# An adaLN attention block: the last V product moved behind the first attention step's scores, the first score tile on other banks, three paired maxima taken singly

## The chip, the core and the metric

The kernel runs on one core of one Trainium2 chip. The time is device time in microseconds (us) for one execution of the whole program, and it is compared as the median of several executions. TensorE, VectorE, ScalarE and GpSimd compute, SyncE (SP) issues most of the transfers. TensorE writes into PSUM, which has eight banks; each 128 x 512 tile of fp32 takes one bank.

## The reference, cut to what matters

```python
# x: 1 x 2048 x 448, 16 heads of 28, feed-forward width 1792, fp32
mod = silu(c) @ w_mod                      # -> sa, ca, ga, sb, cb, gb
h = layernorm(x) * (1 + ca) + sa
q, k, v = split(h @ wqkv)                  # 16 heads
p = softmax((q @ k^T) * 28 ** -0.5)
x = x + ga * ((p @ v) @ wo)
h = layernorm(x) * (1 + cb) + sb
h = gelu(layernorm(h) @ w1 + b1) @ w2 + b2
out = x + gb * h
```

## The kernel before, in words

All products that need more precision than one pass gives are split into a high and a low part, and three of the four part products are summed in PSUM.

**Projection stage** (the loop over `b` from L600). The 2048 tokens are taken in four blocks of 512. For each block a list of tasks is worked off in order: Q and K products of a group of four heads (`qk_task`, L336) and four V products of 128 tokens each (`v_task`, L368), eleven matmuls each (`mm_acc`, L315 to L317). The products write to two PSUM banks named `pa`; ScalarE copies the result out. For the last block (b = 3) the list has six Q and K tasks and then four V products.

**Row maxima.** The softmax takes from each score a bound of its row's maximum, and these maxima are computed ahead, by 32-row matmuls of Q against a chunk of K into banks named `mx` (`max_mm`, L387) with a VectorE reduce for each (`max_one`, L395 to L397). For head group 0 and the later query blocks two key chunks are done as a pair (`pair_diff`, L401): one matmul against the difference of the chunks, a ScalarE Relu (L405), one matmul against the first chunk, and one fused VectorE operation (L409). `emit_task` (L503) puts some of these behind every product of the projection stage: `p1_n` (L526, set in L615 to L621) says how many operations, whether a sixth bank is used, and how many pairs. In the last block each of the first five tasks has one pair at most, each later one three, and nothing is put behind the last V product (L616, L617). All pairs must be done by L677.

**Banks at the handover.** In the projection stage the pool `ps1` holds 2 `pa`, 5 `mx` and 1 `o` bank. It is closed in L680; then the accumulator `o` of attention gets a pool of its own (L683), and `share(3, 2)` (L692) opens a pool with three `mx` banks and two score tiles `s` of two banks each. On SP's queue stand at this place the stores of the last Q and K parts, the loads of the keys of head group 0 (`load_k`, L573), loads of the next group's Q and K (`load_hi`, L416) and of `wo`.

**Attention** (the loop from L1024). Sixteen units (four head groups, four query blocks) of sixteen steps (key tiles of 128). A step makes the scores of four heads in two halves, each into a score tile (L1047), with some maxima between (`emit_max`, L492; four and three in turn in most steps); ScalarE's exponential (L1052) writes them into `pt`, which lies in the slots `c0`, `c1`, `d0` in turn (L1022). The product with V of the step before follows (`av`, L1014 to L1017). The slots `c0` and `c1` held the split input of block 3 in the projection stage, and `d0` the Relu results.

After attention come the output projection's rest and the feed-forward part (L1080 on), which the change doesn't touch.

Of the kernel before, what the change touches and what calls it, by code (L numbers as in the profile page):

```python
# [16 lines left out]
ALU = mybir.AluOpType  # L17
AX = mybir.AxisListType
PSUM = bass.MemoryType.PSUM
# [22 lines left out]
def tile_adaln_block(ctx: ExitStack, tc: tile.TileContext, x, wqkv, wo, w1, b1, w2, b2, c, w_mod, out):  # L42
# [17 lines left out]
    def sbt(tag, shape, dt=F32, bufs=1):  # L60
        return sb.tile(shape, dt, tag=tag, name=nm(tag), bufs=bufs)
# [17 lines left out]
    def ps_s():  # L79
        return psp[0].tile([128, 512], F32, tag="pa", name=nm("pa"), bufs=2)  # L80

    def ps_mx():
        return psp[0].tile([128, 512], F32, tag="mx", name=nm("mx"), bufs=psp[1])
# [281 lines left out]

        return split

    def v_task(b, t):  # L368
        p = ps_s()
        ts = slice(t * 128, (t + 1) * 128)  # L370
        hh, hl = hT[b]
        mm_acc(p[:, :D], terms448(
            lambda k: hh(k)[:, ts], lambda k: hl(k)[:, ts], lambda k: wv[0][:, k, :], lambda k: wv[1][:, k, :],
        ))
        emit_task(*p1_n)
        act.copy(v_sb[b][:, t, :, :DH], p[:, :D].rearrange("p (h d) -> p h d", d=DH))


# [8 lines left out]
    def max_mm(g, qt, i, j, k, ps=None):  # L387
        if (g, qt) not in mxp:
            mxp[(g, qt)] = sbt("mxp", [128, 4, 4, 4], bufs=6)
        m = (ps or ps_mx)()  # L390
        js = slice(32 * j, 32 * j + 32)
        pe.matmul(m, qh_sb[(g, qt)][js, i * 128 : (i + 1) * 128], k[js, :], start=True, stop=True)  # L392
        return m
# [30 lines left out]

    def max_fin(g, qt):
        m32 = sbt("m32", [128, 32], F32R, bufs=2)
        c0 = 1 if (g, qt) in paired else 0
        pool.memset(f(m32)[:, 16:32], 0.0)
        dve.tensor_reduce(
            out=m32[:, 0:16].rearrange("p (h i) -> p h i", i=4),  # L430
            in_=mxp[(g, qt)][:, :, :, c0:].rearrange("p i h c -> p h i c"), op=ALU.max, axis=AX.X, negate=True,
        )

        def put():
            r = sbt("full", [128, 512], F32R, bufs=3)[:, :32]
            dve.transpose(f(r), f(m32))
            dst = f(qst[g * NB + qt])[DH:128:32, 0, :].rearrange("j (i b q) -> j i b q", b=4, q=32)
            for b in range(4):
                sp.dma_start(dst[:, :, b, :], f(r)[32 * b : 32 * b + 16, :])

        late.append([2, put, g * NB + qt])
# [158 lines left out]
    for b in range(NB):  # L600
        more = b + 1 < NB
        tasks = []
        for g in range(1 if b else 0, NG):
            tasks += [(b, 0, g), (b, 1, g)]
        if b == 0:
            tasks[1], tasks[2] = tasks[2], tasks[1]
        tasks += [(b, 2, t) for t in range(4)]
        if more:
            stages, later = stages[-4:] if b else stages, ln1_stages(b + 2) if b + 2 < NB else None
            xs_next = []  # L610
            tasks[10:10] = [(b + 1, 0, 0), (b + 1, 1, 0)]
        for n, (tb, kind, g) in enumerate(tasks):
            post = []
            ready, newq = newq, []
            p1_n[0] = P1RATE if b < 1 else P1RATE + 1  # L615
            if not more and n == len(tasks) - 1:  # L616
                p1_n[0] = 0  # L617

            k = n - (5 if b < 2 else 4)
            p1_n[1] = not (more and (0 <= k < NC)) and not (b == 1 and n < 4)  # L620
            p1_n[2] = (3 if n > 4 else 1) if b == 3 else 2 if b == 2 and p1_n[1] else 1  # L621
            if kind < 2:
                fn = qk_task(tb, kind, g, 6, firsts[n]) if b == 0 and n < 2 else qk_task(tb, kind, g)
                if g == 0:
                    fn()
                else:
                    post.append(fn)
                if kind == 1 and (g == 0 or (g == 1 and tb < 2)):
                    newq = [(g, qt, cch) for qt in range(tb + 1) for cch in range(tb + 1) if max(qt, cch) == tb]
            else:  # L630
                v_task(tb, g)
            for item in ready:
                queue_max(*item)
            if b == 0 and 2 <= n < 6:
                prep_w(2, n - 2, act.copy, dve)
            if more:
                k = n - (5 if b < 2 else 4)
                if b == 0 and n < 4:
                    for fn in stages[2 * n : 2 * n + 2]:
                        fn(xs_next)  # L640
                if b and n < 4:
                    stages[n](xs_next)
                if 0 <= k < NC:
                    post.append(h_chunk(b + 1, xs_next, k))
                if later and 8 <= n < 12:
                    later[n - 8](None)
            if n == 6:
                v_init(b)
                if b == 0:
                    mod_load(0)  # L650
                    mod_load(1)
            if b == 2 and n == 5:
                sp.dma_start(b1_col, b1.rearrange("(k p) -> p k", p=128))
            if b == 1:
                if n < 2:
                    mod_mm(n)
                    mod_load(2 + n)
                elif n in (2, 3):
                    mod_mm(n)
                    if n == 3:  # L660
                        mod_fin()
            if not more:
                if n == 0:
                    load_q(0)
                    load_q(1)
                if n == 5:
                    load_k(0, 0)
                if n == 6:
                    act.activation(cols[:, 0:1], zero_col, AF.Exp)
                    for ch in range(1, 4):  # L670
                        load_k(0, ch)
            tick_late()
            for fn in post:
                fn()
        if more:
            stages = later
    assert not pxq  # L677
    finish_max(0, 0)
    tick_late(True)
    ps1_cm.__exit__(None, None, None)  # L680


    o_pool[0] = ctx.enter_context(tc.tile_pool(name="po", bufs=1, space=PSUM))  # L683
    shared = []

    def share(n_mx, n_s):
        if shared:
            shared.pop().__exit__(None, None, None)
        shared.append(tc.tile_pool(name=nm("ps"), bufs=1, space=PSUM))
        psp[:] = [shared[0].__enter__(), n_mx, n_s]  # L690

    share(3, 2)  # L692

    phase1[0] = False
    for item in deferred:
# [323 lines left out]
                start=(kt == 0), stop=(kt == NKT - 1),  # L1019
            )  # L1020

    ptags = ["c0", "c1", "d0"]  # L1022
    done_max = set()
    for u in range(NU):  # L1024
        g, qt = divmod(u, NB)
        for kt in range(NKT):
            step = u * NKT + kt
            if kt == 1 and u + 1 < NU and u + 1 not in qst:
                load_q(u + 1)
            if kt == NKT - 6 and u + 1 < NU:  # L1030
                finish_max(*divmod(u + 1, NB))
            tick_late()
            if not (three or mxq or late):
                three = True
                share(1, 3)
            pt = slot(ptags[step % 3], [128, 4, 512], F32)
            n = n_maxima(step)
            n0 = 1 if n == 3 and step % 4 == 3 else 2

            ks, qs = kst[(g, kt // 4)], qst[u]  # L1040
            kc = slice((kt % 4) * 128, (kt % 4 + 1) * 128)
            for hf in range(2):
                s2 = ps_s2()
                for term, (kp, qp) in enumerate(((0, 0), (1, 0), (0, 1))):
                    for jj in range(2):
                        rows_ = slice(64 * hf + 32 * jj, 64 * hf + 32 * jj + 32)
                        pe.matmul(s2[:, jj, :], ks[rows_, kp, kc], qs[rows_, qp, :], start=(term == 0), stop=(term == 2))  # L1047
                    if hf == 0 and term < min(n0, n):
                        emit_max(1, 1)
                    if hf == 1 and ((term == 0 and n - n0 > 0) or (term == 2 and n - n0 > 1)):  # L1050
                        emit_max(1, 0)
                act.activation(pt[:, 2 * hf : 2 * hf + 2, :], s2, AF.Exp, scale=SCALE)  # L1052
            if pend is not None:
                pu, pkt, pp, po = pend
                av(pu, pkt, pp, po)
                if pkt == NKT - 1:
                    end_unit(pu, po)
            if kt == 0:
                o = ps_o()
            pend = (u, kt, pt, o)  # L1060
            if qt == NB - 1 and kt % 4 == 3 and g + 1 < NG:
                load_k(g + 1, kt // 4)
            for fn in sched.pop(step, ()):
                fn()
# [90 lines left out]
```

## Time and profile before

| | us |
|---|---|
| median of 3 runs | 1147.98 |
| the runs | 1146.90 to 1148.01 |
| the profiled execution's own time | 1149.55 |
| its span in the profile | 1147.7 |
| TensorE busy in it | 1136.2 |
| mean granted clock of TensorE | 0.997 |

The profile is of one execution. Its lines name engine, line of the kernel, operation, and tiles as output <- input; a group has its count behind an x. "Granted clock" is the share of full speed at which TensorE was let run. In an excerpt in order of time the first column is the start in us from the span's start, the second the length of the group, and in brackets stands idle time before it and what ended that.

### The profile page before, as it was taken

The numbers are of one execution on the slowest core, as the hardware profiler recorded it, in microseconds if no ns is written. First come the engines' busy times: TensorE is split into PE (matmuls) and PEld (weight loads), VectorE is DVE, ScalarE is ACT, GpSimd is POOL, SyncE is SP. The second block draws the span as 40 slices with busy tenths as digits, with TensorE's granted clock in tenths as the row PEclk, the third lists the DMA queues.
The fourth block names the chain that finished last, engine by engine and source line by source line (L and its number), as shares of the span: only waits on it lengthen the run. The fifth ranks groups of instructions, "written<-read, shape, count | busy, mean of one in ns | idle before, by whom it ended". The sixth has DMA issues, their size and how long they took to land.

```text
span 1147.7 us, 20818 instructions
## 1 busy us (share of the span) xinstructions
PE 1136.2 (99%) x8380; PEld 683.8 (60%) x8380; DVE 829.7 (72%) x1487; ACT 682.5 (59%) x839; POOL 216.1 (19%) x232
## 2 busy tenths in 40 slices
PE   8999999999999999999999999999999999999998
PEld 6767765444444444444444444545458888888887
DVE  6868786999999999899999876585438853444322
ACT  4656757778777787878778777675862321211110
POOL 2533431210000000000000011207214503123000
PEclk9999998999999999999999999999999999999999
DMA  9643354121222111222111221020413100000000
GB/s 298 203 145 110 111 178 136 37 56 49 62 75 78 59 47 38 76 75 66 51 44 40 83 84 60 26 84 1 126 55 95 42 33 1 1 33 1 33 1 33
DMA packets 51377, 81.08 MB, mean 71 GB/s; under 512 B 12728, under 2 KB 21772, under 8 KB 51280
## 3 DMA queue, kind: packets, MB, share of 16 engines
q1 hardware_dynamic: 50656, 79.01, 21.8%
q8 instruction: 66, 1.08, 0.4%
q0 software_dynamic: 336, 0.28, 0.1%
q10 hardware_dynamic: 288, 0.46, 0.1%
q14 instruction: 31, 0.25, 0.1%
HBM read 53.11 MB, written 26.35 MB: 69 GB/s over the span
## 4 chain that ended last, share of the span: by engine, by line
PE 96%; DMA 1%; ACT 1%; DVE 1%; issue 0%; DVEq 0%; SPq 0%; ACTq 0%
PE s L1047 28%; PE o L1017 22%; PE mx L317 16%; PE pa L339 7%; PE mx L392 6%; PE s L1105 4%; PE s L1106 4%; PE s L1104 4%; PE pa L317 3%; DMA slot_v<-in_A_wqkv_dram 1%; PE o L240 1%; PE mx L240 1%; ACT slot_c L1052 0%; DMA acc<-in_A_x_dram 0%; PE o L547 0%
## 5 line engine op out<-in xcount | busy, mean ns | idle before, releaser
L397 DVE TENSOR_REDUCE mxp<-mx 128x1 f32<-128x512 f32 x919 | 580.7, 685 | 107.8 <-PE mx L392 103.8
L1047 PE MATMUL s<-slot_b,slot_a 32*128 32x512 f32 x3072 | 384.6, 424 | 1.8 <-ACT full L814 0.7
L1052 ACT ACTIVATE slot_c<-s 128x1024 f32<-128x1024 f32 x342 | 331.7, 1022 | 85.0 <-PE s L1047 84.8
L1047 PEld LDWEIGHTS s<-slot_b,slot_a 32*128 32x128 f32 x3072 | 216.8, 184 | 254.8 <-ACT slot_c L1052 150.8
L392 PE MATMUL mx<-kh,qh 32*128 32x512 f32 x899 | 290.4, 471 | 0.1
L1052 ACT ACTIVATE slot_d<-s 128x1024 f32<-128x1024 f32 x170 | 164.8, 1022 | 42.6 <-PE s L1047 42.5
L1017 PE MATMUL o<-slot_c,v 128*32 128x512 f32 x1368 | 184.4, 608 | 0.4 <-ACT osb L986 0.4
L1088 ACT ACTIVATE full<-mx,b_col 128x512 f32<-128x512 f32 x56 | 38.6, 689 | 192.0 <-PE mx L317 175.6
L1091 DVE CAST hi<-full 128x512 fp32r<-128x512 f32 x56 | 25.2, 450 | 135.4 <-ACT full L1088 135.4
L392 PEld LDWEIGHTS mx<-kh,qh 32*128 32x128 f32 x899 | 116.1, 182 | 5.1 <-DVE mxp L397 3.0
L783 POOL TENSOR_TENSOR osb<-osb,osb 128x512 f32<-128x512 f32 x16 | 21.4, 1336 | 440.8 <-DMA osb<-drec 260.2
L1017 PE MATMUL o<-slot_d,v 128*32 128x512 f32 x680 | 90.6, 605 | 0.0
L1017 PEld LDWEIGHTS o<-slot_c,v 128*32 128x32 f32 x1368 | 27.1, 108 | 57.0 <-issue 54.1
L317 PE MATMUL mx<-y,slot_a 128*128 128x512 f32 x160 | 60.6, 395 | 0.0
L405 ACT ACTIVATE slot_d<-mx 128x512 f32<-128x512 f32 x48 | 27.0, 597 | 40.0 <-PE mx L392 39.9
L1092 DVE TENSOR_TENSOR lo<-full,hi 128x512 fp32r<-128x512 f32 x56 | 43.8, 782 | 5.6 <-DVE hi L1091 0.5
L317 PE MATMUL mx<-y,slot_c 128*128 128x512 f32 x152 | 47.5, 396 | 0.1
L1106 PE MATMUL s<-slot_v,lo 128*128 128x448 f32 x128 | 46.7, 365 | 0.0
L1104 PE MATMUL s<-slot_v,hi 128*128 128x448 f32 x128 | 46.6, 364 | 0.0
L317 PE MATMUL mx<-y,slot_v 128*128 128x512 f32 x112 | 39.2, 396 | 0.0
L317 PE MATMUL mx<-y,slot_b 128*128 128x512 f32 x112 | 39.1, 398 | 0.0
L339 PE MATMUL pa<-slot_c,slot_a 128*128 128x512 f32 x136 | 36.9, 405 | 0.0
(223 smaller groups left out, 1388.4 us busy)
## 6 DMA issues: line engine op xcount, KB each, us to landing
d<-lo SPq DMA_DIRECT2D x32, 256.0 KB
slot_b<-d SPq DMA_DIRECT2D x32, 256.0 KB
slot_a<-d SPq DMA_DIRECT2D x32, 256.0 KB
d<-hi SPq DMA_DIRECT2D x20, 256.0 KB
osb<-drec SPq DMA_DIRECT2D x15, 256.0 KB
out_dram<-xn SPq DMA_DIRECT2D x16, 224.0 KB
slot_v<-in_w_mod_dram SPq DMA_DIRECT2D x4, 784.0 KB
raw<-in_B_w_dram SPq DMA_DIRECT2D x14, 224.0 KB
```

The lines of the kernel that those rows point to most:

```text
L317: pe.matmul(p, a, b, start=(i == 0), stop=(i == len(terms) - 1))
L339: pe.matmul(p, *ts[i], start=(i == 0), stop=(i == len(ts) - 1))
L392: pe.matmul(m, qh_sb[(g, qt)][js, i * 128 : (i + 1) * 128], k[js, :], start=True, stop=True)
L397: dve.tensor_reduce(out=mxp[(g, qt)][:, i, j, cch : cch + 1], in_=m, op=ALU.max, axis=AX.X)
L1017: pe.matmul(o[32 * j : 32 * j + 32, :], v_sb[kt // 4][:, kt % 4, 4 * g + j, :], p[:, j, :], start=(kt == 0), stop=(kt == NKT - 1),)
L1047: pe.matmul(s2[:, jj, :], ks[rows_, kp, kc], qs[rows_, qp, :], start=(term == 0), stop=(term == 2))
L1052: act.activation(pt[:, 2 * hf : 2 * hf + 2, :], s2, AF.Exp, scale=SCALE)
L1088: act.activation(gf, p, AF.Gelu_apprx_tanh, bias=b1_col[:, i : i + 1])
L1092: dve.tensor_tensor(out=glo, in0=gf, in1=f(ghi), op=ALU.subtract)
L1104: pe.matmul(pp, ghi[:, ts], w_hi, start=(m == 0), stop=False)
L1105: pe.matmul(pp, ghi[:, ts], w_lo, start=False, stop=False)
L1106: pe.matmul(pp, glo[:, ts], w_hi, start=False, stop=(m == NFT - 1))
```

## The change

- `v_task` gets its PSUM tile from the caller and calls `emit_task` only in the projection stage.
- The last block's list has three V products. The third, now the last task, writes to an `mx` bank instead of a `pa` bank, and two single maxima stand behind it, no pair.
- The three pairs that are left over at the end of the projection stage are put into the queue of singles, six in all. For that, the first column of a paired block's maxima is preset to a very low number on GpSimd, and the last reduce goes over four columns instead of three.
- The fourth V product, on an `mx` bank, is issued in attention step 0, behind its scores and exponentials, with three maxima behind it.
- The accumulator's pool is opened behind the shared one, on the right side of PSUM, so that the first score tile lies on banks 0 and 1, where the `pa` banks were.
- The `pt` slots rotate from `d0` on, since `c0` and `c1` are read by the moved product.

```diff
-    def v_task(b, t):
-        p = ps_s()
+    def v_task(b, t, p):
...
-        emit_task(*p1_n)
+        if phase1[0]:
+            emit_task(*p1_n)
         act.copy(v_sb[b][:, t, :, :DH], p[:, :D].rearrange("p (h d) -> p h d", d=DH))
...
             mxp[(g, qt)] = sbt("mxp", [128, 4, 4, 4], bufs=6)
+            if (g, qt) in paired:
+                pool.memset(mxp[(g, qt)][:, :, :, 0:1], -3.0e38)
...
-        c0 = 1 if (g, qt) in paired else 0
...
-            in_=mxp[(g, qt)][:, :, :, c0:].rearrange("p i h c -> p h i c"), op=ALU.max, axis=AX.X, negate=True,
+            in_=mxp[(g, qt)].rearrange("p i h c -> p h i c"), op=ALU.max, axis=AX.X, negate=True,
...
-        tasks += [(b, 2, t) for t in range(4)]
+        tasks += [(b, 2, t) for t in range(4 if more else 3)]
...
             if not more and n == len(tasks) - 1:
-                p1_n[0] = 0
+                p1_n[0] = 2
...
-            p1_n[2] = (3 if n > 4 else 1) if b == 3 else 2 if b == 2 and p1_n[1] else 1
+            p1_n[2] = (0 if n == len(tasks) - 1 else 3 if n > 4 else 1) if b == 3 else 2 if b == 2 and p1_n[1] else 1
...
-                v_task(tb, g)
+                v_task(tb, g, ps_mx() if p1_n[0] == 2 else ps_s())
...
-    assert not pxq
+    for g, qt, i, j in pxq:
+        mxq.extend((g, qt, cch, i, j) for cch in range(2))
+    pxq.clear()
     finish_max(0, 0)
     tick_late(True)
     ps1_cm.__exit__(None, None, None)
-    o_pool[0] = ctx.enter_context(tc.tile_pool(name="po", bufs=1, space=PSUM))
...
     share(3, 2)
+    o_pool[0] = ctx.enter_context(tc.tile_pool(name="po", bufs=1, space=PSUM, side="right"))
...
-    ptags = ["c0", "c1", "d0"]
+    ptags = ["d0", "c0", "c1"]
...
                 act.activation(pt[:, 2 * hf : 2 * hf + 2, :], s2, AF.Exp, scale=SCALE)
+            if step == 0:
+                v_task(NB - 1, 3, ps_mx())
+                emit_max(3)
```

## The prediction

> **What bounds the kernel now.** I read the page first, then the time by stretches around the place of the change, then the instructions of TensorE, ScalarE and VectorE there in order of time, and last the order of the built program, which names for each instruction what it waits for. Line numbers are those of the kernel before. First the page: the span, the busy times, and the chain that ended last.
>
> ```profile
> span 1147.7 us, 20818 instructions
> PE 1136.2 (99%) x8380; PEld 683.8 (60%) x8380; DVE 829.7 (72%) x1487; ACT 682.5 (59%) x839; POOL 216.1 (19%) x232
> PE 96%; DMA 1%; ACT 1%; DVE 1%; issue 0%; DVEq 0%; SPq 0%; ACTq 0%
> ```
>
> TensorE is the bound from end to end; all its idle time is 1147.7 - 1136.2 = 11.5 us. The change can win only by taking idle time away or by letting TensorE run faster, and both are looked for where the projection stage hands over to attention. Next the time by stretches of 4 us (columns: TensorE, weight loads, VectorE, ScalarE, GpSimd, then the granted clock, the DMA share and GB/s).
>
> ```profile
> 20.00:24.00 4.00, 2.77 (x10) 1.43 (x9) 3.94 (x8) 1.79 (x5) 0.00 (x0) 1.00 1.06 357
> 176.00:180.00 4.00, 4.00 (x23) 3.21 (x22) 2.79 (x9) 3.18 (x8) 0.00 (x0) 1.00 0.94 174
> 180.00:184.00 4.00, 2.96 (x23) 1.69 (x21) 2.56 (x7) 2.10 (x5) 0.00 (x0) 1.00 1.03 394
> 184.00:188.00 4.00, 3.99 (x23) 1.52 (x23) 2.77 (x5) 2.92 (x3) 0.51 (x1) 0.59 0.63 179
> 188.00:192.00 4.00, 4.00 (x28) 1.67 (x24) 2.53 (x4) 1.94 (x2) 2.59 (x4) 0.56 0.21 55
> 192.00:196.00 4.00, 4.00 (x43) 1.90 (x39) 3.14 (x5) 2.64 (x3) 0.00 (x0) 1.00 0.20 52
> ```
>
> Behind a dip at 180 to 184 us (2.96 of 4 us busy) the granted clock falls to 0.59 and 0.56. At half clock that is (1 - 0.59) x 4 / 0.5 = 3.3 us and 3.5 us: 6.8 us, from about 184.7 to 191.5. This is the hidden cost of the handover. Busy share alone doesn't decide it: at 20 to 24 us TensorE was busy less (2.77) and kept its clock, but on matmuls of 128 rows, while the dip at 181 holds scores of 32 rows. That thin matmuls count for less is my reading of these two rows. Now TensorE in order of time (start, length).
>
> ```profile
> 175.54 2.50 PE L317 MATMUL pa<-slot_e,slot_c 128*128 128x448 f32 x11
> 177.97 0.50 PE L392 MATMUL mx<-raw,qh 32*128 32x512 f32 x3
> 178.73 2.53 PE L317 MATMUL pa<-slot_e,slot_c 128*128 128x448 f32 x11
> 181.88 0.50 PE L1047 MATMUL s<-slot_b,slot_a 32*128 32x512 f32 x2 [0.62 <-ACT v L376]
> 182.68 0.39 PE L392 MATMUL mx<-kh,qh 32*128 32x512 f32 x1
> 183.24 0.49 PE L392 MATMUL mx<-kh,qh 32*128 32x512 f32 x1
> 184.01 0.50 PE L1047 MATMUL s<-slot_b,slot_a 32*128 32x512 f32 x2 [0.28 <-ACT slot_c L1052]
> 186.50 1.94 PE L1017 MATMUL o<-slot_c,v 128*32 128x512 f32 x8
> 188.37 0.79 PE L1047 MATMUL s<-slot_b,slot_a 32*128 32x512 f32 x2
> 192.09 0.49 PE L1047 MATMUL s<-slot_b,slot_a 32*128 32x512 f32 x2
> 193.23 1.07 PE L1017 MATMUL o<-slot_d,v 128*32 128x512 f32 x8
> 194.24 0.50 PE L1047 MATMUL s<-slot_b,slot_a 32*128 32x512 f32 x2
> 197.04 0.50 PE L1047 MATMUL s<-slot_b,slot_a 32*128 32x512 f32 x2
> 199.18 0.50 PE L1047 MATMUL s<-slot_b,slot_a 32*128 32x512 f32 x2
> ```
>
> The third V product starts at 175.54, the last at 178.73; attention steps 0 to 4 start at 181.88, 184.01, 188.37, 192.09 and 194.24. Steady steps take 197.04 - 194.24 = 2.80 (four maxima) and 2.14 us (three). Half clock is seen in the P x V products: 1.94 against 1.07 us. What did the lost clock cost? Without it step 1 would wait for its second exponential (below: 182.94 + 1.94 = 184.88), add 0.8 of scores and 1.0 of P x V, so step 2 at 186.7, step 3 at 189.5, step 4 at 191.6. The drop costs 194.24 - 191.6 = **2.6 us**, and the two gaps 0.62 + 0.28. Those 3.5 us are all that this place holds.
>
> **The change part by part.** The other engines at the place, ScalarE first, then VectorE:
>
> ```profile
> 173.74 0.55 ACT L376 COPY v<-pa 128x448 f32<-128x448 f32 x1
> 174.31 1.28 ACT L669 ACT_TABLE_LOAD   x1
> 175.71 1.56 ACT L405 ACTIVATE slot_d<-mx 128x512 f32<-128x512 f32 x3
> 182.94 1.94 ACT L1052 ACTIVATE slot_c<-s 128x1024 f32<-128x1024 f32 x2 [1.10 <-PE s L1047]
> 177.55 0.69 DVE L409 CUSTOM_DVE_ANT_0 slot_d<-o,slot_d 128x512 f32<-128x512 f32 x1
> 182.49 4.28 DVE L397 TENSOR_REDUCE mxp<-mx 128x1 f32<-128x512 f32 x7 [1.44 <-PE mx L392]
> ```
>
> Seven reduces take 4.28: 0.61 from one to the next, 0.69 for one alone. A reduce starts 182.49 - 181.89 = 0.60 after its matmul's start.
>
> (1) *Third V product on an mx bank.* In the built order it waits for the Relu of the first pair of the group before, since that held the bank. That Relu starts only behind the table load, at 175.71, and takes 0.6: the product starts at 176.33, not 175.54. **+0.8 us**.
>
> (2) *Two singles behind it instead of three pairs.* Product to 178.76, two matmuls of 32 rows, reduces at 179.37 and 179.98, the last done at 180.67. Before, six maxima took 0.7 us of TensorE here; four of them now stand later (three behind the moved product, one at the very end, at most 0.66, the 2.80 less 2.14). Steps without maxima show its likelier price:
>
> ```profile
> 842.87 0.98 PE L1047 MATMUL s<-slot_b,slot_a 32*128 32x512 f32 x12
> 848.83 1.20 PE L1047 MATMUL s<-slot_b,slot_a 32*128 32x512 f32 x12
> ```
>
> Three such steps take 5.96, 1.99 each; seven maxima in two steps cost 4.94 - 3.98 = 0.96, so one costs 0.14. I take that.
>
> (3) *First score tile on banks 0 and 1.* The accumulators left those long before, but the built order still lets the first score wait for the last reduce and the copy of the third product: leaving a pool waits for all of it, as before. So step 0 starts at 180.67 + 0.06 = 180.73, after about 1.4 us of idle TensorE, where before it lost 0.62.
>
> (4) *The moved product* issues eleven matmuls and one copy, no DMA. Attention has three mx banks: the product waits for the second reduce of step 0. With the distances of before (reduce 0.60 after its matmul, both done 1.91 after the step's start) it starts at 180.73 + 1.97 = 182.70; the scores are done at about 182.0, so 0.5 is idle. It ends at 185.2; two singles run at once, the third waits for the product's copy (0.53), to 185.8. Its copy stands between exponentials; ScalarE has room (2.10 of 4 us).
>
> (5) *Step 1* then needs no exponential, which was the wait of 0.28, but each of its three maxima waits for a reduce of one of those singles: reduces end at 186.4, 187.0 and 187.6, so the last scores go at 188.0, P x V at 188.25, step 2 at 189.2. With 2.80 and 2.14 step 4 starts at 194.2, and 0.14 for the late maximum makes it 194.3. At full clock the change thus pays (2.6 of clock won, 2.7 of waits added) **+0.1 us**: nothing.
>
> (6) *Side costs.* Three memsets on GpSimd; VectorE writes other columns and waits for none. The reduce of a unit's maxima goes over 64 instead of 48 elements. Three Relus and three fused reduces go, six plain reduces come; VectorE, 72% busy, takes them. Rows for both sizes and for the memset of a small tile:
>
> ```profile
> 207.22 0.20 DVE L429 TENSOR_REDUCE m<-mxp 128x16 fp32r<-128x48 f32 x1
> 168.74 0.22 DVE L429 TENSOR_REDUCE m<-mxp 128x16 fp32r<-128x64 f32 x1
> 203.78 0.11 POOL L428 MEMSET m<- 128x16 f32 x1
> osb<-drec POOLq DMA_DIRECT2D x1, 256.0 KB, 7.2
> ```
>
> On SP's queue two loads of keys leave the handover for steps 18 and 19, and the key load of step 22 falls to step 24 while its first use stays in step 27: three steps, 7.4 us, against the 7.2 us of the nearest transfer of that size. Nothing, unless it lands later; then its excess.
>
> (7) *Does the clock still fall?* From 178.8 to 182.7 TensorE now runs 18 matmuls of 32 rows and idles about 2 us; from 185.2 to 188.2 again only 18. The first stretch is longer and emptier than the dip that lost the clock before (181.28 to 184.7, idle 0.9, some 25 such matmuls). So I take it that the clock falls again, for about as long, now inside the moved product. Eleven matmuls at 0.22 each become 0.4 or so: +2.0 to +2.4; a part of the scores beside them +0.2 to +0.4; the waits on reduces stay. **+2.2 to +2.8**, and I take 2.5.
>
> Sum: +0.1 + 2.5 = +2.6 us on the profiled execution's 1149.55 (1.85 around its span), so 1152.15. The median of the runs shown lies 1149.55 - 1147.98 = 1.57 below that execution: **1150.6 us**, with 1149.3 to 1151.8 from the bounds above and 0.7 us for distances read from one execution.
>
> By the Trainium skill, "TensorE: Matmul & The Clock Gate", section "Why this matters for your kernels", only gaps of more than about 3 us between bursts cost the clock, so by it neither dip would. The trace here differs: the clock fell behind gaps of 0.62 and 0.28 us, and the measurement decides. The same page's Part 1 has windows of 3.4 us that run freely; the 6.8 us here would be two of them, and by that it is partly chance which dip is caught.
>
> **The rivals.** *The clock stays up.* For it: 2.5 us of full-row matmuls now split the thin stretch in two, and the row at 20 us shows such work keeping the clock at 2.77 of 4. Against: the thin stretch in front of them is emptier than the one that failed. Price: the +0.1 of (5), **1148.0** (1147 to 1149). The page's rule above leads to this time.
>
> *The first score tile really is free, and the clock stays* (the other side). If the handover goes by bank, scores start behind the two singles at about 179.1, 1.6 earlier, while the reduces still run; if in addition the product's wait on the second reduce (0.5 to 0.65) falls behind work, and a part of the chain of step 1 with it, the gain is 2.3 to 3.3: **1145.2**. It decides if step 0 starts before about 179.5. Against it: the two waits that the built order names. This is also the case in which the change does what its title says; my forecast is that it doesn't.
>
> *Two drops.* The thin stretch of step 1 (185.2 to 188.2) loses the clock once more: another 2.6, **1153.2**.
>
> **How the numbers follow.** Within 0.2% means 1145.7 to 1150.3, about what a measurement of this kernel can tell from no change. Forecast (one drop, 1150.6): 0.56, of which 0.37 lies above 1150.3 and 0.19 below. Clock stays: 0.17, within. Free tile: 0.17, faster. Two drops: 0.10, slower. So faster 0.17, within 0.36, slower 0.47. The range 1145.3 to 1152.6 leaves out a good half of the fast case and most of two drops, under 0.2; by itself the likeliest case has 1149.3 to 1151.8.
>
> **What would show it.** Right: the third V product waits for a Relu and starts near 176.3; step 0 starts near 180.7, released by VectorE; the moved product starts about 2 us later, also released by VectorE; the granted clock is about 0.5 for some 7 us from 181.5 to 183.5 on; step 4 starts near 196.8. Wrong: a clock of 1.00 through 176 to 200, a step 0 before 179.5, TensorE waiting for keys near step 27, or a step of attention that is not 2.80 and 2.14 us. I would be wrong on the sign above all if the clock depends on something other than how full the stretch before it was.

## The result, and the profile after

| | before | after |
|---|---|---|
| median | 1147.55 us (6 executions, 1146.73 to 1148.68) | 1151.7 us (6 executions, 1149.91 to 1153.28) |
| ratio of the times | | 1.0036 [1.0025, 1.0047] |
| the profiled execution's own time / span | 1149.55 / 1147.7 us | 1151.32 / 1149.5 us |
| mean granted clock, each execution | 0.996 to 1.000 (the 84 executions beside the experiments) | 0.993 to 0.998 |

The changed kernel is slower by 0.36%, 4.15 us between the medians; 2.6 was forecast. The profiled executions differ by only 1.8 us, the medians by 4.2; why those two differ is the main lesson, and the experiments come back to it. First the page of the changed kernel: span, busy times, the chain that ended last.

```profile
span 1149.5 us, 20814 instructions
PE 1136.1 (99%) x8380; PEld 682.1 (59%) x8380; DVE 832.8 (72%) x1487; ACT 681.3 (59%) x836; POOL 216.5 (19%) x235
PE 96%; DVE 1%; ACT 1%; DMA 1%; issue 1%; DVEq 0%; ACTq 0%
```

TensorE is busy as long as before (1136.1 against 1136.2), so the extra span is idle time: 13.4 against 11.5 us. "Busy" contains half-clock time in both profiles. Next the changed kernel by stretches of 4 us (columns as before: TensorE, weight loads, VectorE, ScalarE, GpSimd, granted clock, DMA share, GB/s).

```profile
20.00:24.00 4.00, 3.13 (x8) 1.86 (x9) 3.94 (x8) 1.53 (x3) 0.00 (x0) 0.83 1.06 362
24.00:28.00 4.00, 4.00 (x15) 3.17 (x14) 3.76 (x12) 0.75 (x2) 1.29 (x1) 0.74 0.96 364
180.00:184.00 4.00, 2.56 (x18) 1.79 (x19) 3.30 (x6) 1.75 (x2) 0.00 (x0) 0.88 1.00 369
184.00:188.00 4.00, 3.81 (x15) 2.83 (x14) 0.67 (x2) 0.72 (x2) 1.57 (x3) 0.69 0.35 82
188.00:192.00 4.00, 3.82 (x36) 1.72 (x36) 3.51 (x7) 1.94 (x2) 1.52 (x3) 1.00 0.30 78
```

The handover is emptier than before (2.56 of 4 us busy, was 2.96). The clock falls at the end of that stretch and in the next: (1 - 0.88) x 4 / 0.5 + (1 - 0.69) x 4 / 0.5 = 0.96 + 2.48 = 3.4 us at half speed, half of what the profile of before lost there. A second drop, not there in the profile of before, lies in 20 to 28, where both kernels run the same matmuls. TensorE in order of time (L1052 scores, L394 maxima, L317 V products, L1022 P x V):

```profile
175.39 0.50 PE L394 MATMUL mx<-raw,qh 32*128 32x512 f32 x3
176.84 2.50 PE L317 MATMUL mx<-slot_e,slot_c 128*128 128x448 f32 x11 [0.72 <-ACT slot_d L407]
179.27 0.50 PE L394 MATMUL mx<-raw,osb 32*128 32x512 f32 x2
181.20 0.50 PE L1052 MATMUL s<-slot_b,slot_a 32*128 32x512 f32 x2 [1.43 <-issue]
183.14 4.01 PE L317 MATMUL mx<-slot_e,slot_c 128*128 128x448 f32 x11
187.77 0.49 PE L394 MATMUL mx<-kh,qh 32*128 32x512 f32 x1 [0.19 <-ACT v L376]
187.77 0.50 PE L1052 MATMUL s<-slot_b,slot_a 32*128 32x512 f32 x2
188.36 0.50 PE L1052 MATMUL s<-slot_b,slot_a 32*128 32x512 f32 x2
188.96 0.71 PE L1052 MATMUL s<-slot_b,slot_a 32*128 32x512 f32 x4
189.56 0.73 PE L1052 MATMUL s<-slot_b,slot_a 32*128 32x512 f32 x4
191.21 0.50 PE L1052 MATMUL s<-slot_b,slot_a 32*128 32x512 f32 x2
196.11 0.50 PE L1052 MATMUL s<-slot_b,slot_a 32*128 32x512 f32 x2
```

The third V product waits 0.72 for a Relu; the first scores stand 1.43 idle; the moved product takes 4.01 instead of 2.50; the last of three singles waits for its copy; the scores of step 1 come 0.59 to 0.60 apart. Step 4 starts at 196.11. ScalarE and VectorE in the changed kernel show what those waits end on:

```profile
174.81 1.28 ACT L671 ACT_TABLE_LOAD   x1
176.21 1.56 ACT L407 ACTIVATE slot_d<-mx 128x512 f32<-128x512 f32 x3
187.18 0.53 ACT L376 COPY v<-mx 128x448 f32<-128x448 f32 x1 [2.99 <-PE mx L317]
```

```profile
179.81 1.29 DVE L399 TENSOR_REDUCE mxp<-mx 128x1 f32<-128x512 f32 x2 [1.06 <-PE mx L394]
181.80 2.48 DVE L399 TENSOR_REDUCE mxp<-mx 128x1 f32<-128x512 f32 x4 [0.70 <-PE mx L394]
187.61 3.68 DVE L399 TENSOR_REDUCE mxp<-mx 128x1 f32<-128x512 f32 x6 [3.33 <-PE mx L394]
```

The two singles' reduces end at 179.81 + 1.29 = 181.10, and step 0 starts 0.10 later, though the profile can only say "issue" there. Six reduces run back to back from 187.61 on; they set the pace of step 1.

### The profile page after: what moved, and what is told of

The parts are those of the page before. It is cut to its first block, busy times and chain, and to the rows that moved or that the text cites. A ratio compares the mean times of both kernels' runs of the same rounds, so it can differ in the third digit from the quotient of the medians.

```text
span 1149.5 us, 20814 instructions
## 1 busy us (share of the span) xinstructions
PE 1136.1 (99%) x8380; PEld 682.1 (59%) x8380; DVE 832.8 (72%) x1487; ACT 681.3 (59%) x836; POOL 216.5 (19%) x235
## 4 chain that ended last, share of the span: by engine, by line
PE 96%; DVE 1%; ACT 1%; DMA 1%; issue 1%; DVEq 0%; ACTq 0%
PE s L1052 28%; PE o L1022 22%; PE mx L317 16%; PE pa L339 7%; PE mx L394 6%; PE s L1113 4%; PE s L1114 4%; PE s L1112 4%; PE pa L317 3%; PE o L240 1%; DMA slot_c<-in_w_mod_dram 1%; PE mx L240 1%; PE o L548 0%; DVE mxp L399 0%; DMA acc<-in_A_x_dram 0%
## 5 line engine op out<-in xcount | busy, mean ns | idle before, releaser
L1052 PE MATMUL s<-slot_b,slot_a 32*128 32x512 f32 x3072 | 383.3, 422 | 2.4 <-issue 1.4
L1057 ACT ACTIVATE slot_c<-s 128x1024 f32<-128x1024 f32 x340 | 329.7, 1022 | 84.6 <-PE s L1052 84.5
L1052 PEld LDWEIGHTS s<-slot_b,slot_a 32*128 32x128 f32 x3072 | 215.4, 183 | 254.0 <-ACT slot_c L1057 149.0
L394 PE MATMUL mx<-kh,qh 32*128 32x512 f32 x901 | 289.0, 469 | 0.6 <-ACT v L376 0.2
L1057 ACT ACTIVATE slot_d<-s 128x1024 f32<-128x1024 f32 x172 | 166.7, 1022 | 43.6 <-PE s L1052 41.6
L1022 PE MATMUL o<-slot_c,v 128*32 128x512 f32 x1360 | 181.2, 605 | 0.0
L394 PEld LDWEIGHTS mx<-kh,qh 32*128 32x128 f32 x901 | 115.6, 182 | 7.4 <-DVE mxp L399 3.7
L1022 PE MATMUL o<-slot_d,v 128*32 128x512 f32 x688 | 92.5, 605 | 0.4 <-ACT osb L991 0.4
L317 PE MATMUL mx<-y,slot_a 128*128 128x512 f32 x160 | 60.6, 395 | 0.0
L1022 PEld LDWEIGHTS o<-slot_c,v 128*32 128x32 f32 x1360 | 26.8, 108 | 54.9 <-issue 53.4
L317 PE MATMUL mx<-y,slot_c 128*128 128x512 f32 x152 | 47.5, 396 | 0.1
L317 PE MATMUL mx<-y,slot_v 128*128 128x512 f32 x112 | 39.2, 396 | 0.0
L317 PE MATMUL mx<-y,slot_b 128*128 128x512 f32 x112 | 39.0, 398 | 0.0
```

Of the source, the lines that this page charges most:

```text
L317: pe.matmul(p, a, b, start=(i == 0), stop=(i == len(terms) - 1))
L1022: pe.matmul(o[32 * j : 32 * j + 32, :], v_sb[kt // 4][:, kt % 4, 4 * g + j, :], p[:, j, :], start=(kt == 0), stop=(kt == NKT - 1),)
```

## The experiments

Theory: at full clock the change adds 2.6 to 2.7 us of waits, and its emptier handover makes the clock fall, in nearly every execution, for 2 to 2.8 us more. Rivals: the clock is not the cause and the waits or the moved maxima cost it all; or the clock falls by chance and as often as before. The experiments keep the clock up with filler matmuls (work that TensorE does in its waits, whose result nobody reads), and undo parts of the change. Beside each median stands in how many executions the mean granted clock was 0.999 or more; one drop of 3.4 us to half speed in some 1148 us makes 0.9985. Of the fourteen profiles, each of the seven at 0.998 or less has such a drop while TensorE works, and none of the seven at 0.999 or more has. A 0.9985 can still be rounded to 0.999, so the counts tell executions with a drop from those without one nearly, not exactly. The kernel before ran beside all of them, 84 executions in three groups: median 1147.2, with 48 of 84 at 0.999 or more, and the 31 at 1.000 have a mean of **1146.46**. That is its time without a drop.

### Fillers in the kernel before

```diff
+    def fill(p, n, r=slice(0, 128)):
+        for _ in range(n):
+            pe.matmul(p[:, :D], wv[0][r, 0, 0:128], wv[0][r, 0, :], start=True, stop=True)
...
     tick_late(True)
+    fill(ps_mx(), 2)
...
+            if step == 0:
+                o = ps_o()
+                fill(o, 2)
```

> The kernel before with four more 128-row matmuls at the handover, whose results nobody reads: two behind the last V product, where TensorE waits for its copy, and two behind the scores of step 0, where it waits for the exponential. My theory (the clock falls because the stretch before it was thin): the granted clock stays at 1.00 from 180 to 196 us, steps 0 and 1 start where they did (181.9 and 184.0), step 4 at about 191.7 instead of 194.2, and the time is about 1145.0 us, 2.5 below before. Rival (the fall has nothing to do with how full the stretch is): the clock falls as before and the time is 1147.5 us or a little above.

The same with 32-row fillers, `slice(0, 32)`:

> The same four added matmuls at the same places, equally long, but with 32 rows instead of 128. If thin matmuls count for less in what the clock follows (my reading of two rows of the profile), the clock falls as in the kernel before and the time stays near 1147.5 us. Rival (idle time alone counts): the clock stays up and the time is that of the 128-row fillers, about 1145.0 us.

Measured: 1146.7 us, 0.9993 [0.9984, 1.0002], clock at 0.999 or more in 10 of 11; with thin fillers 1146.56, 0.9989 [0.998, 0.9997], 9 of 11. TensorE in the kernel before with 128-row fillers:

```profile
175.28 2.50 PE L317 MATMUL pa<-slot_e,slot_c 128*128 128x448 f32 x11
180.81 0.57 PE L452 MATMUL mx<-slot_e 128*128 128x448 f32 x2
181.59 0.49 PE L1052 MATMUL s<-slot_b,slot_a 32*128 32x512 f32 x2 [0.21 <-ACT v L376]
191.44 0.50 PE L1052 MATMUL s<-slot_b,slot_a 32*128 32x512 f32 x2
```

From the third V product to step 4 it takes 191.44 - 175.28 = 16.16 us, against 194.24 - 175.54 = 18.70 in the profile before: a drop of 6.8 us there costs 2.5. But beside its own group (1147.19) the median moved by only 0.5 and 0.6 us, with full fillers not clearly more than nothing, since the kernel before has that drop in a part of its executions only. The expected 1145.0 was missed in both runs for this reason. In this kernel thin fillers do as well as full ones.

### The changed kernel again, and with nine fillers

In front of the handover five, ahead of the moved product two, and two between its second and third single:

```diff
     tick_late(True)
+    fill(ps_mx(), 5)
...
             if step == 0:
+                o = ps_o()
+                fill(o, 2)
                 v_task(NB - 1, 3, ps_mx())
-                emit_max(3)
+                emit_max(2)
+                fill(o, 2)
+                emit_max(1)
```

> The changed kernel with nine 128-row matmuls added in its own waits: five behind the two singles at the handover, two ahead of the moved V product, two ahead of the last of its three singles. My theory (the change adds about 2.7 us of waits, and the clock comes on top): the clock stays up or nearly so, step 0 starts near 180.7 and step 4 near 194.3, and the time is about 1147.7 us, 2.7 above the filled kernel before. Rival (the whole loss of the changed kernel is the clock): as the filled kernel before, about 1145.0 us.

> The changed kernel with the same nine fillers as in the filled changed kernel, at the same places and equally long, but with 32 rows. If idle time alone decides whether the clock falls, the clock stays up and the time is that of the 128-row fillers, about 1149.0 us. If thin matmuls count for less, nine of them lift the longest thin stretch only a little (in the profile of the changed kernel it ran from 179.7 to 183.1 and kept the rows of the array a quarter busy at best), the clock falls in most executions, and the time is 1150.5 to 1151.7 us.

Measured: 128 rows 1148.98 us, 1.0011 [1.0002, 1.002], 11 of 11 at 0.999 or more; 32 rows, on another chip, 1149.66 us, 1.0022 [1.0011, 1.0034], 4 of 8. Between the two kernels with full fillers lie 1148.98 - 1146.7 = 2.3 us, where 2.7 was expected; the times themselves were expected 1.3 and 1.7 too low, by the same 2.5 us of clock that the median did not hold. The thin result lies between both expectations and the chips differ, so both ran once more on one chip, beside the changed kernel itself:

> The changed kernel with nine 128-row fillers in its three waits, once more, so that it stands on one chip beside its thin twin and the changed kernel itself. Theory of waits plus clock: hardly any execution below 0.999, median 2.6 us above the kernel before at full clock (1146.4 to 1146.5), 1149.0, spread within 1 us. Rival (the first result was the luck of a chip): several executions at 0.998 or below and a median of 1149.6 or more.

> The same nine fillers cut to 32 rows, on the same chip as the 128-row ones. If rows count for the clock: at least a third of the executions at 0.998 or below, and a median 0.4 to 2 us above that with 128 rows (1149.4 to 1151). Rival (being busy is what counts, rows don't): clocks and median as with 128 rows, within 0.3 us, 1149.0.

> The changed kernel unaltered, to count in how many executions its clock drops. Theory (its waits make the drop at the handover all but certain): at most one in ten executions at a mean clock of 0.999 or more, median 1151.0 to 1151.8, that is 2.0 to 2.8 above the filled kernel. Rival (the first executions were unlucky, the drop comes in half of them as it does before the change): about half at 0.999 or more, those at about 1149.1, and a median of 1149.5 to 1150.3.

| on one chip | median us | ratio to before | clock 0.999 or more |
|---|---|---|---|
| changed kernel | 1151.63 | 1.0041 [1.0028, 1.0054] | 0 of 6 |
| with nine 32-row fillers | 1151.52 | 1.0033 [1.0021, 1.0045] | 0 of 5 |
| with nine 128-row fillers | 1149.72 | 1.0019 [1.001, 1.0029] | 8 of 9 |

The clock counts fit the theory in all three, though the thin fillers' median lies above the expected 1149.4 to 1151. The full fillers' median is 0.7 above the first group's 1148.98: two groups of one program differ by that much.

TensorE with 128-row fillers (here L1057 is the scores, L453 the fillers):

```profile
175.90 2.50 PE L317 MATMUL mx<-slot_e,slot_c 128*128 128x448 f32 x11 [0.74 <-ACT slot_d L407]
178.76 1.29 PE L453 MATMUL mx<-slot_e 128*128 128x448 f32 x5
180.36 0.49 PE L1057 MATMUL s<-slot_b,slot_a 32*128 32x512 f32 x2 [0.31 <-PE mx L453]
182.63 2.39 PE L317 MATMUL mx<-slot_e,slot_c 128*128 128x448 f32 x11
193.99 0.50 PE L1057 MATMUL s<-slot_b,slot_a 32*128 32x512 f32 x2
```

With 32-row fillers:

```profile
176.93 2.50 PE L317 MATMUL mx<-slot_e,slot_c 128*128 128x448 f32 x11 [0.72 <-ACT slot_d L407]
179.37 0.50 PE L394 MATMUL mx<-raw,osb 32*128 32x512 f32 x2
179.37 1.29 PE L453 MATMUL mx<-slot_e 32*128 32x448 f32 x5
181.40 0.49 PE L1057 MATMUL s<-slot_b,slot_a 32*128 32x512 f32 x2 [0.73 <-DMA raw<-in_A_wo_dram]
183.34 4.05 PE L317 MATMUL mx<-slot_e,slot_c 128*128 128x448 f32 x11
196.35 0.50 PE L1057 MATMUL s<-slot_b,slot_a 32*128 32x512 f32 x2
```

Both have step 0 4.46 or 4.47 us behind the start of the third V product, the changed kernel 4.36: fillers shorten no wait. Yet the moved product takes 2.39 with the full ones, and step 4 follows the third product by 193.99 - 175.90 = 18.09, against 196.35 - 176.93 = 19.42 with the thin ones and 196.11 - 176.84 = 19.27 without. The difference is the clock, less what the full fillers themselves cost (below). (The releaser "DMA" in the thin case is only the semaphore that came last by the profile; the start is no later than with the full ones.) That rows alone decide is not shown: the thin fillers start together with the singles (both at 179.37) and run beside them, while the full ones start 0.43 behind them (178.33 and 178.76), so the thin ones leave 0.73 idle where the full ones leave 0.31.

The first run of the thin fillers was profiled in an execution that kept its clock:

```profile
176.19 2.50 PE L317 MATMUL mx<-slot_e,slot_c 128*128 128x448 f32 x11 [0.74 <-ACT slot_d L407]
189.17 0.50 PE L1057 MATMUL s<-slot_b,slot_a 32*128 32x512 f32 x2
```

From the third product to step 2 it takes 189.17 - 176.19 = 12.98 us; the same program with the drop takes 191.45 - 176.93 = 14.52. So a drop of 3.4 us inside the moved product costs 1.5 us. With full fillers and the clock kept the stretch takes 189.08 - 175.90 = 13.18.

The changed kernel's second profile lost its clock at another place:

```profile
184.00:188.00 4.00, 3.63 (x24) 1.80 (x22) 2.44 (x5) 1.06 (x2) 2.34 (x3) 1.00 0.22 56
188.00:192.00 4.00, 4.00 (x26) 1.58 (x24) 2.42 (x5) 1.77 (x3) 0.75 (x2) 0.57 0.42 103
```

```profile
176.27 2.50 PE L317 MATMUL mx<-slot_e,slot_c 128*128 128x448 f32 x11 [0.72 <-ACT slot_d L407]
182.56 2.53 PE L317 MATMUL mx<-slot_e,slot_c 128*128 128x448 f32 x11
185.72 0.50 PE L1052 MATMUL s<-slot_b,slot_a 32*128 32x512 f32 x2
188.16 1.86 PE L1022 MATMUL o<-slot_d,v 128*32 128x512 f32 x8
195.52 0.50 PE L1052 MATMUL s<-slot_b,slot_a 32*128 32x512 f32 x2
```

Here the moved product kept its clock (2.53), and the P x V of step 0, behind the thin stretch with the singles' waits, ran at half (1.86 for 1.06). (1 - 0.57) x 4 / 0.5 = 3.4 us again, and again 195.52 - 176.27 = 19.25 to step 4. So the handover offers the drop two places. Since this profile kept its clock up to step 1 and the first one had it back from there on, the two together give the changed kernel without fillers at full clock: 185.72 - 176.27 = 9.45 to step 1, and 196.11 - 187.77 = 8.34 from there to step 4, together 17.79. Against that each drop costs about 1.5 us, and the full fillers, with 18.09, cost 0.3 themselves.

### Undoing parts of the change

The third V product back on a `pa` bank, all else (with the nine fillers) as changed:

```diff
-                v_task(tb, g, ps_mx() if p1_n[0] == 2 else ps_s())
+                v_task(tb, g, ps_s())
```

> The filled changed kernel with the third V product on its accumulator bank again. My theory (the mx bank costs the wait for the Relu behind the table load): that product starts 0.7 us earlier, and everything behind it; about 1148.3 us, 0.7 below the filled changed kernel. Rival (the wait is hidden, since step 0 waits for later things anyway): as the filled changed kernel, 1149.0 us.

The same and no singles behind the third product (two fillers in place of five):

```diff
-                p1_n[0] = 2
+                p1_n[0] = 0
```

> The one before, with no maxima behind the third V product (two more are left for attention), and two fillers instead of five. My theory (step 0 waits for the last reduce because the pool is left as a whole): step 0 starts about 0.6 us behind the product's end, 1.35 us earlier, and the two maxima cost 0.3 later: about 1147.3 us. Rival (the first score tile is free, and something else holds step 0): no gain, 1148.3 us or 0.3 more.

Measured 1148.12 us, 1.0007 [0.9998, 1.0016], and 1147.6 us, 1.0001 [0.9992, 1.001], both near what was expected. Executions at a clock of 1.000, against those of the kernel before on the same chip: the filled changed kernel 1149.14 - 1146.56 = +2.6 and, in its second group, 1149.55 - 1146.42 = +3.1; without the `mx` bank 1147.88 - 1146.36 = +1.5; without the singles too 1147.07 - 1146.36 = +0.7. By these means the bank costs 1.1 to 1.6 us (between two chips), the two singles in front of the handover 0.8 (on one). For the bank the traces show 0.8 of it. TensorE with the product back on `pa`:

```profile
175.86 0.50 PE L394 MATMUL mx<-raw,qh 32*128 32x512 f32 x3
176.53 2.50 PE L317 MATMUL pa<-slot_e,slot_c 128*128 128x448 f32 x11
189.71 0.50 PE L1057 MATMUL s<-slot_b,slot_a 32*128 32x512 f32 x2
```

The third product starts 0.67 behind the start of the maxima ahead of it, in the changed kernel 176.84 - 175.39 = 1.45 behind; from the product to step 2 it takes 13.18 us, as with the `mx` bank and the same fillers. The rest of the 1.1 to 1.6 is no more than the two means of the filled changed kernel differ by (2.6 and 3.1). TensorE without the singles too:

```profile
174.69 2.50 PE L317 MATMUL pa<-slot_e,slot_c 128*128 128x448 f32 x11
177.81 0.50 PE L1057 MATMUL s<-slot_b,slot_a 32*128 32x512 f32 x2 [0.22 <-ACT v L376]
```

Step 0 now follows the third product by 3.12 us instead of 4.46, and waits only for that product's copy: no reduce stands in its way. With the singles, and the product on either bank, it starts 0.1 to 0.2 behind the last reduce.

### The moved product on the output bank

As above without fillers; the moved product writes the accumulator's bank, which is free until step 1, and no singles stand behind it:

```diff
             if step == 0:
-                v_task(NB - 1, 3, ps_mx())
-                emit_max(3)
+                v_task(NB - 1, 3, ps_o())
```

> The changed kernel without the three choices that add waits: the third V product goes to its accumulator bank again, no maxima stand behind it, and the moved product goes to the accumulator of attention, which is free until step 1, so that it waits for no reduce and nothing waits for its copy. No filler. My theory (the place behind the scores is good, the banks chosen for it are not): step 0 near 178.7, step 1 near 182.7, step 4 near 190, the clock up, since the full product stands close behind the thin scores; about 1144.0 us. Rival (the place itself costs, by the exponentials or by maxima moved out of the projection stage): 1147.5 us or more.

Measured 1145.6 us, 0.998 [0.9971, 0.9989]: 0.2% faster than the kernel before, and faster than the changed one; the clock was at 0.999 or more in 7 of 11, not always up as expected, and the expected 1144.0 was not reached. At a clock of 1.000 it is 1145.39 - 1146.56 = -1.2 against before. TensorE:

```profile
179.31 0.50 PE L1052 MATMUL s<-slot_b,slot_a 32*128 32x512 f32 x2 [0.62 <-ACT v L376]
181.09 2.53 PE L317 MATMUL o<-slot_e,slot_c 128*128 128x448 f32 x11
183.54 0.50 PE L1052 MATMUL s<-slot_b,slot_a 32*128 32x512 f32 x2
185.68 0.50 PE L1052 MATMUL s<-slot_b,slot_a 32*128 32x512 f32 x2
```

Step 1 starts as the product ends and takes a steady 2.14 us. Between +0.7 and -1.2 lie three changes at once (the moved product's bank, the singles behind it, the fillers), and another chip; which of them brings how much was not separated. The same with two fillers at the handover and, in one version, eight short ones in the load stage (not shown here):

```diff
     tick_late(True)
+    fill(ps_mx(), 2)
```

> The version with the moved product on the accumulator bank of attention, with two fillers at the handover and eight short ones in the waits of the first 24 us, where its profile lost the clock for 3.4 us. My theory: the granted clock is 1.00 in nearly all executions and the median is that version's at full clock, about 1145.2 us, with less scatter. Rival (the fillers delay what they fill): 1145.6 us or more.

> The cheapest arrangement so far (moved product on the output bank, third V product on the scores' bank, no singles behind the moved product), with two 128-row filler products at the handover only. If the moved product's dense stretch is what keeps the clock here and the handover's 1.4 us of thin work and waits is the last weak place: nearly every execution at a mean clock of 0.999 or more, median about 1145.4 beside 1147.4 for the kernel before (ratio 0.998 to 0.9985), and no execution at 0.997 or below. Rival: the fillers cost what the clock gives back: 1145.6 to 1146.7, no better than the same kernel without fillers.

Measured: with early fillers 1146.71 us, 0.9991 [0.9982, 0.9999], clock at 0.999 or more in 11 of 11; with the two at the handover alone 1145.33 us, 0.9987 [0.9978, 0.9995], 8 of 11, where the version without fillers had 7 of 11. The intervals overlap: the fillers bring nothing here that can be told from no gain, and no execution was at 0.997 or below. At a clock of 1.000 the version with early fillers is 1146.60 - 1146.36 = +0.2 against before on its chip, where the one without any was -1.2: its rival, that the fillers delay what they fill, fits better than the theory, though the two stand on different chips.

## Why the prediction was right or wrong

Forecast: slower, 1150.6 us. Measured: 1151.7. The waits at the handover went as worked out; the bookkeeping of the clock did not.

(1) to (4) and the waits of (5) hold. Everything in the first profile of the changed kernel is 0.5 us late already at the third V product (176.84, forecast 176.33); that lies ahead of the change, where the profile has its early drop, and the other profiles with this bank put that start anywhere from 175.74 to 176.93. Less that 0.5: last reduce 180.6 (180.67), step 0 180.69 (180.73), moved product 182.63 (182.70). Step 1's scores keep the reduces' pace, and step 2 follows step 1 by 3.44 (3.4). At full clock the changed kernel takes 17.79 us from the third product to step 4, put together from its two profiles; forecast 194.2 - 176.33 = 17.87. The wait of (1) is 1.45 - 0.67 = 0.8 us (both above), as forecast. The waits in all were put at 2.7 us; the filled kernels show 2.6 and 3.1, of which the fillers themselves are about 0.3. Why step 0 waits for the last reduce is argued from the built order; the runs show that it does, and that it starts earlier when no reduce is there.

(6) holds: no wait of TensorE for a key load appears, and busy TensorE time is unchanged.

**The step that failed is the subtraction of 1.57 us** in the sum, beside the "2.6 of clock won" in (5): they take the same drop off twice. I took the drop of one profile for a property of every execution. It was in that profile, and cost 2.5 there (forecast 2.6), so 1149.55 - 2.6 = 1146.95 is already near the 1146.46 without a drop. The 1.57 by which the profiled execution stood above the median was mostly that same drop, and I took it off a kernel that has its own. Against the median the change could not win 2.6: 48 of 84 executions of before have a mean clock of 0.999 or more, only 24 are as low as the profiled one (0.997 or less), and the medians (1147.2 and 1147.55) are only 0.8 to 1.1 above 1146.46. With that time as the base the forecast's own terms give 1146.5 + 2.7 + 2.5 = 1151.7. That this is the measured time is partly luck, as (7) shows.

(7) was right that the clock falls, and its size came out near by luck. I had one drop of 7 us inside the moved product, +2.5, and step 4 near 196.8. The runs show drops of 3.4 us, inside that product or behind it, about 1.5 each at this place; step 4 stands at 196.11, less the 0.5 at 195.6. None of 12 executions is at 0.999 or more. Between the medians the clock costs 1151.63 - 1149.72 = 1.9 on one chip, and against the first filled kernel 1151.7 - 1148.98 = 2.7 across groups, in both cases against kernels whose fillers cost 0.3. So more than one such drop is common; nine of the twelve are at 0.997 or less. One other place is known: five of the fourteen profiles, the first of the changed kernel among them, have a drop between 22 and 28 us. Where the rest lies stays open.

My reading that thin matmuls count for less stood on the row at 20 to 24 us, where 128-row matmuls kept the clock. It does not bear it: those five profiles lost the clock in that very stretch of 128-row matmuls (in the first of the changed kernel 0.83 and 0.74, above), so keeping it was a matter of the execution. Fillers support the reading in the changed kernel and not in the kernel before; it is not settled.

The rivals. *The clock stays* is what the filled kernel shows, and it gives 1149.0 to 1149.7, not 1148.0: by the same error, since the waits were set off against a clock that was up in more than half of the executions anyway. The rule behind that rival (the Trainium skill, "TensorE: Matmul & The Clock Gate", "Why this matters for your kernels") fails here: the clock fell behind gaps of 1.43 and less. The traces fit Part 1 of that page of the Trainium skill: freely running windows of 3.4 us agree with drops of 3.4 and 6.8 us at differing places. *The first tile free*: it was not, as forecast. The time that I gave it, 1145.2, is reached when the handover no longer waits for reduces and the product's bank is free: 1145.3 and 1145.6. *Two drops*: single executions reach its time, 1153.28 at a mean clock of 0.993, but they were not profiled, so where their drops lay is not known.

## What to carry to other kernels

Before pricing a clock drop from a profile, look at the mean clock of every execution: a drop in the profiled one may be in a part of them only, and a distance between profile and median may be that drop, so it must not be counted twice. Before moving a dense product into a gap, see that its bank is free and that nothing behind it waits for its copy or for reduces: here the move cost 2.6 to 3.1 us at full clock (0.3 of it fillers) on a shared bank with singles around it, and won 1.2 on a bank of its own without them.

## What the runs showed of the hardware

Drops were of 3.4 us (the changed kernel) or 6.8 (the profile of before), at half speed (granted clock 0.50 from 186 to 190 us in the profile of before), and began at different places in equal programs (at 183 us in one profile of the changed kernel, at 188 in the other). In these profiles no gap of TensorE in the 6 us ahead of a drop was longer than 1.43 us, and drops came in 128-row work alone (22 to 28 us) as well as behind 32-row work. One drop at the handover cost about 1.5 us. Nine 128-row fillers in the waits kept the clock in 19 of 20 executions without shortening any wait and cost about 0.3 us themselves; nine 32-row ones kept it in 4 of 13. Fillers of 32 rows started together with singles of 32 rows (both at 179.37), those of 128 rows 0.43 behind them.
